# Chunked attention and expert layers on one core: another order for the first 20 microseconds of set-up

## The chip, the core and the metric

The kernel runs on one core of a Trainium2 chip. The core has a matmul engine (TensorE, in the profile PE, with the loading of its stationary operand as PEld), three engines for elementwise work (VectorE or DVE, ScalarE or ACT, GpSimd or POOL), and SyncE (SP), whose queue issues nearly all loads here. The metric is the device time of one execution in microseconds (us). The time before is 486.27 us, the median of three runs (484.25 to 487.78).

## The reference

Two parts follow each other. The first is attention in chunks of 32 tokens, with 16 tokens of context on the left, 8 on the right, and 8 memory keys and values for each head:

```python
B, H, S, D = 4, 8, 768, 64
for c in range(S // 32):
    l, r = max(0, c * 32 - 16), min(S, c * 32 + 32 + 8)
    k_full = np.concatenate([mem_k, k[:, :, l:r]], axis=2)
    v_full = np.concatenate([mem_v, v[:, :, l:r]], axis=2)
    s = D ** -0.5 * np.matmul(q[:, :, c * 32:c * 32 + 32], k_full.transpose(0, 1, 3, 2))
    a = np.exp(s - s.max(-1, keepdims=True))
    a = a / (a.sum(-1, keepdims=True) + 1e-9)
    out[:, :, c * 32:c * 32 + 32] = np.matmul(a, v_full)
```

The second takes the 3072 tokens with 512 features each, finds the best of 8 experts for each token (a softmax over x @ w_gate), places up to `capacity` tokens in each expert, computes relu(x @ w1) @ w2 for them (512 to 1024 to 512), and multiplies by the token's gate value.

## The kernel before

Attention works through 24 tiles of 128 tokens, two to a segment of 256 tokens. For each segment there is a key tile KW (two buffers, named kw in the profile), which holds for each chunk the 64 columns that a chunk of queries meets: 24 shared with the chunk before, 32 of its own, 8 of memory keys. Two heads share a tile: head parity 0 has rows 0 to 63, parity 1 rows 64 to 127, and the other half of each block of columns has to be zero. The value tile VW (two buffers, vw) is built in the same way, with a column of ones that gives the sum of the exponentials.

For each segment, queries and keys are loaded on SP's queue (`load_q` L357, `load_k` L368), turned by PE (`trans_q` L463, `trans_k` L475), and copied from PSUM to SBUF by ACT, in the first segment partly by DVE (L465, L479). `copy_k` copies the shared keys from chunk to chunk and into the next key tile (L496, L498), and in the first segment of a batch the eight keys that come before (L492). `fill_mem_k` copies the memory keys into both key tiles of a batch (L450); they come from preT, which `trans_pre` makes out of the loaded memory keys with eight small transposes on PE (L433) and four copies (L437). `load_v` (L397, L400) loads values into VW, and `fill_mem_v` (L426) copies memory values by DMA from the tile ME, which POOL builds out of the loaded memory values, memv (L167 to L172).

Each engine carries out its instructions in the order in which the program has them; no planner moves them. What is changed is the part between the first load and the loop over tiles. In it the unused halves are cleared: `zero_k` (L128) copies zeros from the tile pad into a key tile, `zero_v` clears half of a value tile (L135 by POOL, L137 by ACT) and sets its ones (L138). `dummy` (L150) issues matmuls on zeros (two entries of the profile for each). The order before is:

- SP: keys 0, queries 0 (each in two halves), memory keys with the eight first keys of each head (`load_mem`, L118 and L119), memory values (L123), keys 1, queries 1, values 0, memory rows of VW 0, keys 2, queries 2, memory rows of VW 1, values 1.
- PE: dummies, keys 0, queries 0, memory keys, 20 dummies, and then the loop: scores of tile 0 (`scores`, L509), keys 1, scores of tile 1, queries 1, the transposes of tile 0's exponentials (L533), scores of tile 2, keys 2, and the first value product (`value`, L550).
- DVE: clearing of KW 0, its half of keys 0, its half of queries 0, then `copy_k`, its half of `fill_mem_k`, the clearing of half of KW 1 (`zero_k(1, 0)`), and in the loop a half of `fill_mem_k(1)`, the maximum of tile 0 (L517), the subtraction (L520), and the shared keys of segment 1.
- ACT: clearing of half of VW 0, its halves of keys 0 and queries 0, the four copies of `trans_pre`, its half of the shared and the memory keys; in the loop the four copies of keys 1.
- POOL: half of VW 0, ME, the other half of KW 1 (L173), both halves of VW 1, and at the loop's start its half of `fill_mem_k(1)`, without which the scores of tile 2 can't start; then the constants of the routing (from L578).

The loop starts each tile with scores, then the transposes of the next segment, the exponentials, and the later stages of earlier tiles. The expert part comes behind attention and is not touched.

## Time and profile before

| | |
|---|---|
| median of three runs | 486.27 us (484.25 to 487.78) |
| the profiled execution's own time | 483.69 us |
| its span, first to last instruction | 481.8 us |
| PE busy | 458.3 us (95%) |
| DVE busy | 308.9 us (64%) |
| ACT busy | 232.6 us (48%) |
| POOL busy | 118.2 us (25%) |
| mean granted clock of PE | 0.993 |

The shares are means over the whole span. The set-up is the first 13 us, the attention loop goes on to about 135 us, and the experts take the rest. In the timeline a row gives the start, the time from the start of its first to the end of its last instruction, engine, line, operation, the tiles written and read, the sizes, the count of instructions, and in brackets the idle time before it with what ended it. Rows of one engine can overlap by some hundredths of a microsecond. Rows marked SPq are issues of DMAs, with the waits inside them; not the transfers.

### The profile page before, as it was taken

What the parts mean: (1) busy time and instruction counts of PE and PEld (TensorE: products, weight loads), DVE (VectorE), ACT (ScalarE), POOL (GpSimd) and SP (SyncE); (2) the same over time, 40 slices, a digit from 0 to 9 for tenths busy, and PEclk for the clock granted to TensorE, in tenths of its full rate; (3) what the DMA queues carried; (4) which work ended last, traced back from release to release, by engine and by line L of the source; (5) the groups of instructions that cost most, each with busy time, mean ns of one, the idle gap of its engine ahead of it and who ended that gap; (6) DMA issues with size and microseconds to landing.
All of it is one profiled execution on the core that took longest, in us unless ns stands there. A gap on an engine that the chain in (4) does not pass through costs nothing.

```text
span 481.8 us, 11847 instructions
## 1 busy us (share of the span) xinstructions
PE 458.3 (95%) x4317; PEld 386.9 (80%) x4317; DVE 308.9 (64%) x686; ACT 232.6 (48%) x423; POOL 118.2 (25%) x158
## 2 busy tenths in 40 slices
PE   7899999999999999979999999999999999899993
PEld 6777877878789897867777898899888878677782
DVE  5988899999869447565448257555624676674410
ACT  6587968889635235255345056244502544533200
POOL 8631245555543621201001100100021011020011
PEclk9899999999999999999999999999999999999998
DMA  9787788897976755365705554270414356430011
GB/s 214 150 216 189 184 209 245 249 246 186 230 252 236 263 167 193 105 224 180 237 34 181 173 190 133 88 267 16 164 53 149 123 187 229 163 131 3 1 42 44
DMA packets 79920, 78.85 MB, mean 164 GB/s; under 512 B 33394, under 2 KB 60142, under 8 KB 79792
## 3 DMA queue, kind: packets, MB, share of 16 engines
q1 hardware_dynamic: 74992, 62.33, 44.4%
q0 software_dynamic: 4800, 14.95, 8.1%
q8 instruction: 65, 1.06, 1.0%
q14 instruction: 63, 0.52, 0.3%
HBM read 61.25 MB, written 15.99 MB: 160 GB/s over the span
## 4 chain that ended last, share of the span: by engine, by line
PE 52%; DMA 18%; issue 13%; DVE 10%; ACT 2%; SPq 1%; POOLq 1%; DVEq 0%; ACTq 0%
PE ps L858 19%; DMA out_dram<-y,tok 13%; PE ps L948 13%; PE lgp L927 5%; DMA raw<-in_q_dram 3%; PE ps L834 2%; PE ps L550 2%; DVE vw L415 2%; PE ps L463 2%; PE ps L509 2%; PE ps L331 2%; ACT kw L479 1%; DVE m L517 1%; DVE d L520 1%; SPq L397 1%
## 5 line engine op out<-in xcount | busy, mean ns | idle before, releaser
L871 ACT ACTIVATE hhi<-ps 128x512 fp32r<-128x512 f32 x68 | 40.7, 599 | 148.6 <-PE ps L858 133.0
L955 POOL DMA_INDIRECT out_dram<-y,tok x28 | 32.3, 1155 | 273.3 <-DVEq L842 140.9
L872 DVE SCALAR_TENSOR_TENSOR hlo<-ps,hhi 128x512 fp32r<-128x512 f32 x68 | 47.0, 691 | 68.6 <-ACT hhi L871 65.7
L858 PE MATMUL ps<-xhi,w1hi 128*128 128x320 f32 (+3 forms) x288 | 59.5, 328 | 3.6 <-ACT w2hi L849 1.7
L948 PE MATMUL ps<-w2hi,hhi 128*128 128x512 f32 x152 | 60.9, 401 | 0.0
L948 PE MATMUL ps<-w2lo,hhi 128*128 128x512 f32 x152 | 59.8, 393 | 0.0
L948 PE MATMUL ps<-w2hi,hlo 128*128 128x512 f32 x152 | 59.4, 391 | 0.0
L858 PE MATMUL ps<-xhi,w1lo 128*128 128x320 f32 (+3 forms) x288 | 57.7, 322 | 0.0
L858 PE MATMUL ps<-xlo,w1hi 128*128 128x320 f32 (+3 forms) x288 | 57.7, 322 | 0.0
L858 PEld LDWEIGHTS ps<-xhi,w1hi 128*128 128x128 f32 x288 | 45.2, 188 | 8.3 <-issue 2.1
L858 PEld LDWEIGHTS ps<-xhi,w1lo 128*128 128x128 f32 x288 | 45.9, 188 | 2.9
L858 PEld LDWEIGHTS ps<-xlo,w1hi 128*128 128x128 f32 x288 | 45.9, 188 | 2.8
L954 DVE TENSOR_SCALAR y<-ps,xg 128x512 f32<-128x512 f32 x19 | 14.3, 751 | 51.6 <-PE ps L948 44.0
L850 DVE TENSOR_TENSOR w2lo<-raw,w2hi 128x512 fp32r<-128x512 f32 x64 | 41.2, 685 | 0.9 <-DVEq L919 0.6
L823 DVE TENSOR_TENSOR w1lo<-raw,w1hi 128x512 fp32r<-128x512 f32 x56 | 36.7, 684 | 2.7 <-DVEq L842 0.8
L822 ACT CAST w1hi<-raw 128x512 fp32r<-128x512 f32 (+1 forms) x72 | 37.1, 573 | 0.9
L849 ACT CAST w2hi<-raw 128x512 fp32r<-128x512 f32 x64 | 36.2, 617 | 1.6 <-DMA raw<-in_moe_w_dram 1.6
L838 ACT CAST xhi<-ps 128x512 fp32r<-128x512 f32 x34 | 19.8, 587 | 29.6 <-PE ps L834 26.3
L948 PEld LDWEIGHTS ps<-w2hi,hlo 128*128 128x128 f32 x152 | 28.6, 188 | 6.7
L948 PEld LDWEIGHTS ps<-w2hi,hhi 128*128 128x128 f32 x152 | 28.5, 188 | 6.7
L839 DVE TENSOR_TENSOR xlo<-ps,xhi 128x512 fp32r<-128x512 f32 x34 | 23.1, 689 | 16.7 <-ACT xhi L838 16.7
L948 PEld LDWEIGHTS ps<-w2lo,hhi 128*128 128x128 f32 x152 | 28.5, 188 | 5.8
(169 smaller groups left out, 814.6 us busy)
## 6 DMA issues: line engine op xcount, KB each, us to landing
raw<-in_moe_w_dram SPq DMA_DIRECT2D x15, 2048.0 KB
raw<-in_q_dram SPq DMA_DIRECT2D x11, 512.0 KB
raw<-in_k_dram SPq DMA_DIRECT2D x10, 512.0 KB
vw<-in_v_dram SPq DMA_DIRECT2D x49, 64.0 KB
xg<-x_d SPq DMA_DIRECT2D x3, 792.0 KB
vw<-in_v_dram SPq DMA_DIRECT2D x31, 72.0 KB
xg<-x_d SPq DMA_DIRECT2D x4, 528.0 KB
xg<-x_d SPq DMA_DIRECT2D x2, 1056.0 KB
```

The costliest lines, as they stand in the source:

```text
L822: self.nc.scalar.copy(out=hi[sl], in_=raw[sl])
L823: (eng or self.nc.vector).tensor_tensor(out=lo[sl], in0=raw[sl], in1=hi[sl].bitcast(F32), op=ALU.subtract)
L838: nc.scalar.copy(out=self.xhi[:, d:d + k, sl], in_=pv)
L839: nc.vector.tensor_tensor(out=self.xlo[:, d:d + k, sl], in0=pv, in1=self.xhi[:, d:d + k, sl].bitcast(F32), op=ALU.subtract)
L849: self.nc.scalar.copy(out=self.w2a[:, j], in_=self.raw2[:, j])
L850: self.nc.vector.tensor_tensor(out=self.w2b[j // 4][:, j % 4], in0=self.raw2[:, j], in1=self.w2a[:, j].bitcast(F32), op=ALU.subtract)
L858: self.nc.tensor.matmul(ps, a[:, d, fs], b[:, d, o:o + w], start=(i + d == 0), stop=(i == 2 and d == KD - 1))
L871: self.nc.scalar.activation(out=self.hhi[hs], in_=ps, func=AF.Relu)
L872: self.nc.vector.scalar_tensor_tensor(out=self.hlo[hs], in0=ps, scalar=0.0, in1=self.hhi[hs].bitcast(F32), op0=ALU.max, op1=ALU.subtract)
L927: nc.tensor.matmul(ps, a, b, start=start, stop=stop)
L948: self.nc.tensor.matmul(ps, a[:, f, t * P:t * P + P], b, start=(f == 0 and i == 0), stop=(f == KF - 1 and i == 2))
L955: nc.gpsimd.indirect_dma_start(out=self.out[:, :], out_offset=bass.IndirectOffsetOnAxis(ap=tok[:, t:t + 1], axis=0), in_=y, in_offset=None ...
```

## The change

The load of the memory keys goes ahead of the first queries on SP's queue. On PE the memory keys are turned before the queries, and 20 dummies become 6, behind them. `copy_k` is cut in two, `share_k` (shared keys) and `prior_k` (the eight keys before); in the set-up the shared keys are copied right behind `trans_k(0)`, the others behind `trans_pre`. Two of the four copies of `trans_pre` go from ACT to DVE, DVE's half of `fill_mem_k(0)` goes to POOL, and `zero_k(1, 0)` from DVE to ACT. On POOL the clearing of half of KW 1 and of ME comes first, and `zero_v(0, 1)` comes behind the memory keys. On SP keys 2 and queries 2 come ahead of the memory rows of VW 0, and values 1 ahead of the memory rows of VW 1. In the loop the order and the engines are as before.

```diff
         self.load_k(0)
+        load_mem()
         self.load_q(0)
-        load_mem()
         load_memv(0)
...
         zero_v(0, 0, nc.scalar.copy)
-        zero_v(0, 1, None)
         self.load_v(0)
-        self.trans_k(0)
-        self.trans_q(0)
-        self.trans_pre(pre)
-        dummy(20)
-        self.copy_k(0)
-        self.fill_mem_k(0)
-        zero_k(1, 0)
+        nc.gpsimd.memset(KW[1][64:P, :, :, 0, :].rearrange("p a c d -> p (a c) d"), 0.0)
         nc.gpsimd.memset(ME, 0.0)
         for par in range(2):
             nc.gpsimd.memset(ME[par * 32:par * 32 + 32, par, :, 64:65], 1.0)
+        self.trans_k(0)
+        self.share_k(0)
+        self.trans_pre(pre)
+        self.prior_k(0)
         for par in range(2):
             r = slice(par * 32, par * 32 + 8)
             nc.gpsimd.tensor_copy(out=ME[r, par, :, 0:64], in_=memv[r])
-        nc.gpsimd.memset(KW[1][64:P, :, :, 0, :].rearrange("p a c d -> p (a c) d"), 0.0)
-        self.fill_mem_v(0)
+        self.trans_q(0)
         self.load_k(2)
         self.load_q(2)
+        self.fill_mem_k(0)
+        dummy(6)
+        zero_k(1, 0, nc.scalar.copy)
+        zero_v(0, 1, None)
+        self.fill_mem_v(0)
+        self.load_v(1)
         zero_v(1, 0, None)
         zero_v(1, 1, None)
         self.fill_mem_v(1)
-        self.load_v(1)
...
         for j in range(2):
             for hf in range(2):
-                nc.scalar.copy(out=self.preT[...], in_=ps[...])
+                (nc.vector.tensor_copy if hf else nc.scalar.copy)(out=self.preT[...], in_=ps[...])
...
-            (self.nc.scalar.copy if n == 0 and not hf else (self.nc.gpsimd if n and not hf else self.nc.vector).tensor_copy)(
+            (self.nc.scalar.copy if n == 0 and not hf else (self.nc.gpsimd if not n or not hf else self.nc.vector).tensor_copy)(
                 out=kw[r, :, :, hf, 56:64], in_=self.pre_cols(0, b)[r, :, None, :].broadcast_to([64, 4, 8, 8]))
...
     def copy_k(self, n):
+        self.prior_k(n)
+        self.share_k(n)
+
+    def prior_k(self, n):
         nc = self.nc
         b, s = self.segs[n]
-        kw, kx = self.KW[n % NKW], self.KW[(n + 1) % NKW]
         if s == 0:
             for hf in range(2):
                 r = slice(hf * 64, hf * 64 + 64)
-                nc.vector.tensor_copy(out=kw[r, :, 0, hf, 16:24], in_=self.pre_cols(1, b)[r])
+                nc.vector.tensor_copy(out=self.KW[n % NKW][r, :, 0, hf, 16:24], in_=self.pre_cols(1, b)[r])
+
+    def share_k(self, n):
+        nc, s = self.nc, self.segs[n][1]
+        kw, kx = self.KW[n % NKW], self.KW[(n + 1) % NKW]
         for hf in range(2):
             r = slice(hf * 64, hf * 64 + 64)
             copy = nc.scalar.copy if n == 0 and not hf else (nc.vector if n <= 1 or hf else nc.gpsimd).tensor_copy
             copy(out=kw[r, :, 1:8, hf, 0:24], in_=kw[r, :, 0:7, hf, 32:56])
             if s < NSEG - 1:
                 copy(out=kx[r, :, 0, hf, 0:24], in_=kw[r, :, 7, hf, 32:56])
```

## The prediction

> **What bounds the kernel now.** I read the page first, for the share of the matmul engine, then the busy times of stretches of 12 us, then the chain of waits and the timeline of the first 24 us, where the whole change lies. The page's head and the stretches:

> ```profile
> span 481.8 us, 11847 instructions
> ...
> 0.00:12.00 12.00, 9.36 (x110) 8.03 (x110) 7.02 (x11) 7.73 (x12) 9.97 (x18) 1.00 0.92 214
> 12.00:24.00 12.00, 10.37 (x181) 8.80 (x185) 11.57 (x20) 6.93 (x12) 7.48 (x15) 0.86 0.71 151
> 24.00:36.00 12.00, 11.52 (x246) 9.55 (x239) 10.72 (x29) 10.75 (x17) 3.79 (x11) 1.00 0.83 216
> ```

> After the length the columns are PE, PEld, DVE, ACT and POOL busy, PE's clock, the share of the DMA engines and GB/s. From 24 us on PE and DVE are nearly full. Before that PE has 12.00-9.36 = 2.6 and 12.00-10.37 = 1.6 us of idle time, and its clock is below full in the second stretch, where DVE (11.57) is the full engine. What ends last there, from the chain of waits:

> ```profile
> 1.77 4.61 DMA raw<-in_q_dram
> ...
> 10.65 2.07 DVE kw L492
> ...
> 13.51 3.04 DVE kw L128
> ...
> 17.17 0.70 DVE m L517
> ```

> The set-up waits for the first queries, then DVE carries the path. Two DVE entries are far too long for what they do: the copy of a 64x32 block takes 2.07 us, and clearing half of the second key tile 3.04. Both are copies from SBUF to SBUF that lie beside a POOL clearing of the second value tile. The timeline, with POOL's rows first:

> ```profile
> 7.90 0.84 POOL L172 COPY ME<-memv 8x256 f32<-8x256 f32 x2 [1.12 <-DMA memv<-in_mem_v_dram]
> 8.80 1.80 POOL L173 MEMSET kw<- 64x2048 f32 x1
> 10.64 2.05 POOL L135 MEMSET vw<- 64x2340 f32 x1
> 13.23 2.23 POOL L135 MEMSET vw<- 64x2340 f32 x1
> 15.42 1.24 POOL L138 MEMSET vw<- 64x36 f32 x1
> 16.71 0.71 POOL L450 COPY kw<-preT 64x256 f32<-64x256 f32 x1
> ...
> 13.63 1.14 PE L509 MATMUL ps<-kw,qT 128*32 128x128 f32 x32 [1.93 <-DVE kw L450]
> 14.70 1.97 PE L475 MATMUL ps<-ident,raw 128*128 128x128 f32 x8
> 16.60 1.70 PE L509 MATMUL ps<-kw,qT 128*32 128x128 f32 x32
> 18.23 1.97 PE L463 MATMUL ps<-ident,raw 128*64 128x128 f32 x32
> 20.71 1.08 PE L509 MATMUL ps<-kw,qT 128*32 128x128 f32 x32
> 21.73 1.09 PE L475 MATMUL ps<-ident,raw 128*128 128x128 f32 x8
> 23.18 1.11 PE L550 MATMUL ps<-vw,pT 128*32 128x130 f32 x32
> ```

> The short DVE copy ends at 10.65+2.07 = 12.72, as POOL's clearing ends at 10.64+2.05 = 12.69; the DVE clearing has only 1.1 us left after 13.23+2.23 = 15.46. So a DVE copy within SBUF waits for a POOL clearing that began first. PE's first scores start at 13.63 after 1.93 us of idle time, and their maximum is taken only at 17.17, behind that DVE clearing. The first scores of the second segment (of 256 tokens; segment 1, as segments count from 0) start at 20.71. That is the point at which I compare, because from there PE and DVE are both full.

> **The change, part by part.** All times are on the clock of this trace.

> ```profile
> 2.87 0.50 SPq L118 DMA_DIRECT2D raw<-in_mem_k_dram  x1
> 3.88 0.70 SPq L123 DMA_DIRECT2D memv<-in_mem_v_dram  x2
> 14.71 0.39 SPq L368 DMA_DIRECT2D raw<-in_k_dram  x1
> 16.74 2.24 SPq L426 DMA_DIRECT2D vw<-ME  x2
> 19.04 6.22 SPq L397 DMA_DIRECT2D vw<-in_v_dram  x8
> 3.85 1.62 PE L475 MATMUL ps<-ident,raw 128*128 128x128 f32 x8
> 7.51 0.85 PEld L463 LDWEIGHTS ps<-ident,raw 128*64 128x64 f32 x16 [0.24 <-DMA raw<-in_q_dram]
> 8.54 0.68 PE L433 MATMUL ps<-ident,raw 32*128 32x32 f32 x8
> 9.15 2.55 PE L150 MATMUL ps<-pad 128*64 128x64 f32 x40
> 8.66 0.69 DVE L465 COPY qT<-ps 128x512 f32<-128x512 f32 x1 [1.75 <-PE ps L463]
> 13.11 0.37 DVE L450 COPY kw<-preT 64x256 f32<-64x256 f32 x1
> 18.50 0.57 DVE L496 COPY kw<-kw 64x672 f32<-64x672 f32 x1
> 2.04 2.14 ACT L137 COPY vw<-pad 64x2340 f32<-64x2340 f32 x1
> 9.25 1.09 ACT L437 COPY preT<-ps 64x128 f32<-64x128 f32 x4 [1.06 <-PE ps L433]
> 10.37 0.75 ACT L496 COPY kw<-kw 64x672 f32<-64x672 f32 x1
> 11.20 0.62 ACT L450 COPY kw<-preT 64x256 f32<-64x256 f32 x1
> 15.85 2.52 ACT L479 COPY kw<-ps 64x512 f32<-64x512 f32 x4 [4.03 <-PE ps L475]
> ```

> *Memory keys before queries.* On SP's queue the queries move behind two issues that took from 2.87 to 3.88. At most they come 3.88-2.87 = 1.0 us later; at least by the bytes, 0.131 MB at 214 GB/s = 0.6. A gain is excluded: nothing moves out of their way. I take 0.8, so the second half of the queries, which PE waited for until 7.51, comes at 8.3. The memory keys take the queries' place in the queue, so they are there by 1.77+4.61 = 6.4, and their eight transposes (0.68) fit into PE's wait after 3.85+1.62 = 5.5. The later loads keep their places and bytes.

> *Order on PE.* Query transposes ended at 8.54; now 8.54+0.8 = 9.3, DVE's copy of the second half (0.69) at about 10.1. The warming matmuls shrink from 40 to 12, 2.55*12/40 = 0.8 us, and lie beside that copy.

> *Key tile 0.* ACT leaves its key copies at about 6.3 (they don't depend on anything moved). The shared keys cost it 11.20-10.37 = 0.8, two quarters of the 1.09 for the transposed memory keys 0.5, its query copy runs at about 8.4 to 9.0, the memory columns 0.62: done at 9.7. DVE does the shared keys (0.57 and one short copy, POOL being without a clearing there), two copies from PSUM and the 64x32 blocks by 9.0. POOL's memory copies end at 8.74 as before (they wait for a load whose place is kept), then it does its new half of the memory columns, 0.71 by the POOL row at 16.71: 9.5. So the first scores start at about 10.2, when the queries' copy is done, instead of 13.63.

> *Clearing on ACT.* The 3.04 us leave DVE. ACT clears 64x2048, by its row for 2340 columns 2.14*2048/2340 = 1.9 us, from 9.7 to 11.6. Behind it wait ACT's four key copies of segment 1 (2.52), whose first PE block would be ready at about 11; so 0.6 at most, covered by DVE, which is busy with the first maximum until then. If that cover is gone it costs 0.6.

> *DVE.* Its first instruction of the loop is a memory-column copy (0.37), which finds POOL clearing from 9.5 and waits until 9.5+2.05 = 11.6. The first maximum then starts at about 12.3 instead of 17.17: 4.9 earlier.

> *POOL, which is late next.* All three value clearings still stand ahead of POOL's half of the memory columns of segment 1, at 16.71 in the trace. The first one went from the front to behind the wait for the memory values, and the 0.71 is new. From 9.5: three clearings with their columns of ones, at best 3*2.2 = 6.6, and 0.71, which ends at 16.8. Its conflicts with DVE come on top: DVE's memory column (0.37) and four shared copies of segment 1 (two of 0.57 and two short ones, about 1.5) can hold POOL for up to 1.9: 18.7. The shortest case is excluded by the row at 15.42, where a small memset beside a DVE copy took 1.24 us. I take 18.2, and scores of segment 1 from 18.3 instead of 20.71. **The sum is 20.71-18.3 = 2.4 us**, with ends of 2.0 (18.7) and 3.9 (16.8).

> [...] If each of POOL's clearings won against the four shared copies, the end of 18.7 would hold and the sum be 2.0, not my 18.2 and 2.4.

> *SP.* The same number of issues stands in the set-up; it ended at 19.04+6.22 = 25.26. The second value load no longer stands behind the memory rows of the second tile, whose issue took 2.24 with its wait for POOL. So SP ends between 0 and 2.2 us earlier, which agrees with the sum. Behind it the third key load and all later loads move with it. The first tile's memory rows now stand behind two loads of 0.5 MB each, of which below.

> From 20.7 us on, no instruction changes; the 2.4 us should stay. The profiled execution took 483.69 us, its span 481.8 and 1.9 around it: 481.3 by the sum. It lies 2.6 below the median of 486.27, so against the median the forecast is **483.9**.

> **The rivals.** *The clock falls again (485.4).* After 1.93 us of idle PE the clock went to half:

> ```profile
> 15.00:16.00 1.00, 1.00 (x6) 1.00 (x5) 1.00 (x1) 0.15 (x1) 1.00 (x2) 0.50 0.45 58
> ```

> [...] It cost 1.97-1.09 = 0.9 on key transposes and 1.70-1.08 = 0.6 on scores, 1.5 in all, while DVE was the path anyway. In the changed kernel PE runs scores, transposes and scores (1.1 each from 10.2) and query transposes (1.97) until about 15.5, then four transposes, and then waits for POOL's 18.2: again some 2 us idle, and now PE itself is late afterwards. 2.4-1.5 = 0.9 is left. For it: the same idle length. Against: the fall need not follow each time; the idle time before 6.4 brought none (1.00 in the first stretch).

> *All of it passes (481.4).* POOL is done at its early end, and later stalls shrink too, as loads start earlier; one such stall:

> ```profile
> 91.20 8.55 DMA raw<-in_q_dram
> ```

> Then DVE's 4.9 us are kept: 481.4. Against it: POOL's early end excludes every conflict.

> *Nothing passes (486.3).* That load at 91.20 is one of several on the chain; if the DMA engines set the pace there, what the start gains is given back. Against: their share of 0.83 at 24 to 36 leaves room. This is also the case in which the reordering doesn't do what it says.

> *Slower: memory rows behind the loads (488.8).* The two copies of memory rows into value tile 0 had been issued before the load at 14.71; now they follow two loads of 0.52 MB. The first value product (23.18) needs them, and PE takes its work in order, so the scores and products of the next tiles queue behind. Two loads at the 151 GB/s of that stretch take 6.9 us; from 14 that is 21, in time. If the rate were that of its worst parts, near 100, they'd take 10.5 and the product would start at 24.5 or later, 1.3 late; with the clock falling in that new wait, 1.5 more: some 2.5 slower. It decides where the rows land after 23.18. [...] No row here shows the order of these landings.

> **How the numbers follow.** Forecast 0.42, clock 0.22, all passes 0.16, nothing 0.10, slower 0.10. The likeliest is 483.9. One per cent is 4.9 us, about what can be told from no change here (three runs lay between 484.25 and 487.78). Faster by more: most of the third case, whose 4.9 is just at the bound, and the far end of the forecast with 3.9: 0.16. Slower by more (over 491.1): only the far end of the last case, and scatter: 0.07. Within: 0.77. The range runs from 481.0, a little past the third case, to 488.5, just short of the slower one; its own range for the forecast alone is 482.4 to 484.3.

> **What would show it.** First scores at about 10 and first maximum at about 12.3; no DVE clearing of the second key tile; POOL's memory columns of segment 1 ending near 18, and the second segment's scores right behind them, with PE idle for 2 us before. Wrong would be: scores of segment 1 waiting for something else than POOL, the first value product waiting for memory rows, or a shift at 24 us that is gone by 130.

## The result, and the profile after

The changed kernel takes 491.16 us (median of four runs, 490.51 to 492.63) against 485.26 us for the kernel before, run beside it (four runs, 484.23 to 487.78). The ratio is 1.0125, with a 95% interval from 1.009 to 1.016: **1.25% slower**, where 483.9 us, 0.5% less than the 486.27 known then, was forecast. Executions of a kernel that took far longer than its others (735.37 us in one below) enter no ratio. The profiled execution took 491.75 us with a span of 490.0, against 483.69 and 481.8: 8.2 us more between the first and the last instruction.

Nothing of this was lost in the set-up, where the whole reordering lies. From the page of the changed kernel, and then its busy times by stretches of 12 us (the columns are those of the table that the prediction shows):

```profile
span 490.0 us, 11790 instructions
...
PE 462.1 (94%) x4289; PEld 390.0 (80%) x4289; DVE 306.1 (62%) x686; ACT 233.7 (48%) x422; POOL 117.4 (24%) x159
...
q8 instruction: 65, 1.06, 0.9%
```

```profile
0.00:12.00 12.00, 10.20 (x80) 9.25 (x81) 7.15 (x15) 8.54 (x11) 8.64 (x17) 1.00 0.88 216
12.00:24.00 12.00, 11.12 (x221) 8.92 (x219) 9.77 (x16) 8.48 (x15) 8.92 (x18) 1.00 0.75 165
24.00:36.00 12.00, 9.71 (x197) 7.97 (x194) 9.64 (x26) 8.65 (x14) 2.81 (x8) 1.00 0.81 197
```

The page of the kernel before has, for the line with the engines' busy times:

```profile
PE 458.3 (95%) x4317; PEld 386.9 (80%) x4317; DVE 308.9 (64%) x686; ACT 232.6 (48%) x423; POOL 118.2 (25%) x158
```

From 12 to 24 us PE does 221 matmuls where it did 181, as the change meant it to. From 24 to 36 us it does 197 where it did 246: the lead is gone again. PE has 4317-4289 = 28 matmuls fewer in the whole program, and as many loads of its stationary operand: the 14 warming calls that were dropped, four PE instructions each, 56 in all. That number mattered more than the order.

The timeline of the changed kernel, the rows that answer to those of the prediction:

```profile
7.52 3.68 PE L465 MATMUL ps<-ident,raw 128*64 128x128 f32 x32
10.99 1.49 PE L150 MATMUL ps<-pad 128*64 128x64 f32 x12
12.41 1.15 PE L520 MATMUL ps<-kw,qT 128*32 128x128 f32 x32
18.25 1.45 PE L520 MATMUL ps<-kw,qT 128*32 128x128 f32 x32
22.14 1.10 PE L561 MATMUL ps<-vw,pT 128*32 128x130 f32 x32 [0.57 <-DMA vw<-ME]
31.53 1.06 PE L477 MATMUL ps<-ident,raw 128*128 128x128 f32 x8 [2.29 <-DMA raw<-in_k_dram]
34.59 1.08 PE L520 MATMUL ps<-kw,qT 128*32 128x128 f32 x32
127.40 1.11 PE L520 MATMUL ps<-kw,qT 128*32 128x128 f32 x31
...
13.89 0.69 DVE L528 TENSOR_REDUCE m<-ps 128x8 f32<-128x512 f32 x1
...
10.57 1.90 ACT L128 COPY kw<-pad 64x2048 f32<-64x2048 f32 x1
...
17.58 0.61 POOL L452 COPY kw<-preT 64x256 f32<-64x256 f32 x1
...
16.57 6.07 SPq L398 DMA_DIRECT2D vw<-in_v_dram  x8
24.31 1.82 SPq L123 DMA_DIRECT2D memv<-in_mem_v_dram  x2
26.23 0.39 SPq L369 DMA_DIRECT2D raw<-in_k_dram  x1
```

The same rows of the kernel before, as far as the prediction does not have them:

```profile
26.10 0.39 SPq L368 DMA_DIRECT2D raw<-in_k_dram  x1
...
30.47 1.06 PE L475 MATMUL ps<-ident,raw 128*128 128x128 f32 x8
33.98 1.08 PE L509 MATMUL ps<-kw,qT 128*32 128x128 f32 x32 [0.36 <-DVE kw L492]
127.60 1.11 PE L509 MATMUL ps<-kw,qT 128*32 128x128 f32 x31
```

The scores of segment 1 (tile 2) start at 18.25 instead of 20.71, right behind POOL's memory columns, which end at 17.58+0.61 = 18.19. Tile 3 is only 1.1 us ahead (23.03 against 24.10): the scores of tile 2 ran 1.45 us instead of 1.08, and PE waited 0.20 us for ACT and 0.57 us for the memory rows of VW 0. Tile 4 is 1.2 us ahead. Then the transposes of segment 3's keys wait 2.29 us for a load that was issued at 26.23, as before (26.10), and tile 5 starts 0.6 us later than before (34.59 against 33.98). At the last tile of attention 0.2 us are left (127.40 against 127.60). So attention ends where it ended, and the 8.2 us come behind it, in the expert part, whose code the change does not touch. Four stretches of 10 us there, first of the kernel before, then of the changed one:

```profile
200.00:210.00 10.00, 9.03 (x75) 8.61 (x74) 6.70 (x11) 6.31 (x12) 1.10 (x1) 1.00 0.83 281
210.00:220.00 10.00, 8.33 (x56) 7.16 (x55) 6.16 (x10) 4.36 (x9) 0.00 (x0) 1.00 0.51 169
370.00:380.00 10.00, 9.64 (x65) 9.15 (x64) 6.78 (x12) 6.08 (x11) 0.00 (x0) 1.00 0.73 268
380.00:390.00 10.00, 10.00 (x58) 8.01 (x57) 7.18 (x13) 6.25 (x12) 0.00 (x0) 1.00 0.38 121
```

```profile
200.00:210.00 10.00, 6.94 (x56) 6.49 (x55) 5.13 (x9) 4.35 (x8) 0.91 (x1) 1.00 0.87 278
210.00:220.00 10.00, 8.20 (x51) 7.24 (x50) 6.06 (x10) 4.93 (x9) 0.00 (x0) 0.87 0.35 103
217.00:221.00 4.00, 3.71 (x14) 3.08 (x14) 1.05 (x3) 0.59 (x1) 0.00 (x0) 0.57 0.61 143
370.00:380.00 10.00, 7.64 (x52) 7.24 (x51) 6.35 (x10) 4.45 (x8) 1.14 (x1) 1.00 0.74 250
380.00:390.00 10.00, 9.51 (x52) 9.23 (x53) 3.55 (x6) 3.43 (x7) 0.00 (x0) 0.83 0.14 50
381.00:385.00 4.00, 4.00 (x19) 4.00 (x18) 0.69 (x1) 0.60 (x1) 0.00 (x0) 0.57 0.08 30
```

From 200 to 210 us PE loses 9.03-6.94 = 2.1 us of busy time and 19 matmuls; from 370 to 380 us, 2.0 and 13. The clock falls twice, from 217.41 and from 381.25 us, each time from 1.00 to 0.50 for 3.41 us by the trace's records. The second fall follows the end of a stop of 2.85 us at 380.49; the first doesn't follow the stop near 206 us directly, but a later one of 1.80 us:

```profile
217.29 0.51 PE L938 MATMUL lgp<-w2lo,hhi 128*128 128x512 f32 x1 [1.80 <-issue]
```

In the kernel before the clock doesn't fall in the experts until their last 3 us. The 0.57 over 4 us agrees: (1-0.57)*4/0.5 = 3.4 us of it were at 0.50. What a fall costs is an estimate: by the ratio of the two clocks, 3.4 us at 0.50 stand for at least 1.7 at 1.00, so each fall costs up to 1.7 (eight key transposes of the kernel before took 1.97 us in a stretch where the clock went down to 0.50, and 1.09 at 1.00, a factor of 1.8). What PE waits for, from the timeline of the changed kernel around 206 us:

```profile
205.33 0.71 PE L869 MATMUL ps<-xhi,w1hi 128*128 128x256 f32 x4 [0.25 <-DVE hlo L883]
208.85 0.74 PE L869 MATMUL ps<-xhi,w1lo 128*128 128x256 f32 x4 [2.81 <-issue]
```

And of the kernel before at the same point of the program:

```profile
205.52 0.71 PE L858 MATMUL ps<-xhi,w1hi 128*128 128x256 f32 x4 [0.25 <-DVE hlo L872]
206.07 0.63 PE L858 MATMUL ps<-xhi,w1lo 128*128 128x256 f32 x4
...
214.07 0.33 PE L867 MATMUL ps<-pad 128*64 128x64 f32 x2 [1.67 <-issue]
```

PE stops in the middle of a row of matmuls for 2.81 us, and the releaser is "issue": no tile, no load and no other engine that this view knows of. (What moves beside it is looked at in the last experiment.) The kernel before has such stops too, at other points, here 1.67 us ahead of the matmuls on zeros at 214.07 (the program has them in the other arm of a branch, for where tokens are skipped). If all idle times of PE above 0.3 us behind 150 us are added up from the two timelines, it is 5.9 us before (6 of them) and 11.4 after (7 of them). The difference of 5.5, and two falls of the clock at 1.7, less the 0.2 that attention gained, make 8.7 us, where the span grew by 8.2; the 0.5 too much isn't traced further.

### The profile page after: what moved, and what is told of

Its sections match the earlier page's. It is cut to its first block, busy times and chain, and to the rows that moved or that the text cites. A ratio compares the mean times of both kernels' runs of the same rounds, so it can differ in the third digit from the quotient of the medians.

```text
span 490.0 us, 11790 instructions
## 1 busy us (share of the span) xinstructions
PE 462.1 (94%) x4289; PEld 390.0 (80%) x4289; DVE 306.1 (62%) x686; ACT 233.7 (48%) x422; POOL 117.4 (24%) x159
## 3 DMA queue, kind: packets, MB, share of 16 engines
q8 instruction: 65, 1.06, 0.9%
## 4 chain that ended last, share of the span: by engine, by line
PE 54%; DMA 19%; issue 14%; DVE 7%; ACT 2%; POOL 1%; POOLq 1%; SPq 0%; DVEq 0%; ACTq 0%
PE ps L869 18%; DMA out_dram<-y,tok 13%; PE ps L959 13%; PE lgp L938 5%; DMA raw<-in_k_dram 3%; PE ps L561 3%; PE ps L845 2%; PE ps L520 2%; PE ps L465 2%; DMA raw<-in_q_dram 2%; PE ps L332 1%; PE ps L616 1%; DMA vw<-ME 1%; DVE vw L416 1%; PE lgp L959 1%
## 5 line engine op out<-in xcount | busy, mean ns | idle before, releaser
L481 ACT COPY kw<-ps 64x512 f32<-64x512 f32 x46 | 28.8, 626 | 10.2 <-PE ps L477 8.9
```

Source lines behind the costliest of these rows:

```text
L481: (nc.vector.tensor_copy if n == 0 and hf else nc.scalar.copy)(out=kw[r, :, :, hf, 24 + j:56:2], in_=ps[j * 64:j * 64 + 64])
```

## The experiments

Three theories stood at the start. *Order* (rival B in the expectations): the new order of the set-up is itself the cause, through the loads that now start at other times and the memory rows behind two big loads, with something of it reaching the experts. *Warming* (rival C): the missing warming calls cost by themselves, at the start. *Position* (theory A): the cause is that PE's program has 56 instructions fewer ahead of the experts, so that everything behind lies at another place relative to the blocks in which, by this theory, PE's instructions are fetched. The page of the profile bears on this with the queue q8 of kind "instruction", which moved 1.06 MB in 65 packets, 16 KB each. In the first 140 us of the kernel before one of them starts on average for every 252 PE instructions of the profile (5034 for 20 packets), behind 150 us of the changed kernel one for every 76 (3439 for 45). That such a packet is a block of PE's instructions, of about 252 of them, is an estimate from the first of these figures; the packets themselves are looked at in the last experiment. The expert part has branches (tiles without tokens are skipped), attention has none.

### Both orders, with 20 and with 6 warming calls

The changed kernel with the 20 calls of the kernel before:

```diff
-        dummy(6)
+        dummy(20)
```

> The changed kernel with 20 warming matmuls instead of 6 behind the first queries, as many as before, so PE has as many instructions ahead of the experts as before. Theory A (code position): PE's stalls in the expert part come from where its instructions lie in the blocks of 16 KB that it fetches, and return to those of before: after 172 us no stall of 2.8 us, some 6 us of stalls in all instead of 11, clock not falling at 217 and 381; total 484 to 487 us. Rival B (time): the expert part is disturbed because attention's loads and releases come at other moments; then the stalls stay near 11 us and the total at 490 to 492. Rival C (fewer warming matmuls): the missing warming itself costs; it would show in the first 20 us alone, with a gain there, and leave the expert part at 490.

The kernel before with 6 calls, its order untouched:

```diff
-        dummy(20)
+        dummy(6)
```

> The kernel before with one edit, 6 warming matmuls instead of 20. Theory A: the expert part gets the stalls of the changed kernel (one of 2.8 us near 206, one near 378), total 489 to 492 us though nothing else of the change is there. Rival B: 485 to 487, stalls as before. Rival C: a slower first 20 us (clock low longer), up to 2 us, the expert part as before.

The times, as ratios to the kernel before (485.2 us, run beside them; for the changed kernel the 485.26 of the result), with 95% intervals:

| | 20 calls | 6 calls |
|---|---|---|
| order before | 1 | 1.0119 (1.0038 to 1.0199) |
| order after | 1.0012 (0.9977 to 1.0048) | 1.0125 (1.009 to 1.016) |

The loss goes with the 14 calls and not with the order. Dropping the calls alone makes the old order slower by as much as the whole change; with the calls put back, the new order can't be told from the old one. The timeline of the new order with 20 calls, at the point where the changed kernel stopped for 2.81 us:

```profile
205.84 0.63 PE L869 MATMUL ps<-xhi,w1lo 128*128 128x256 f32 x4
...
213.85 0.33 PE L878 MATMUL ps<-pad 128*64 128x64 f32 x2 [1.38 <-issue]
```

The stop is gone from there, and stands ahead of the matmuls on zeros, as in the kernel before. The old order with 6 calls:

```profile
206.53 0.72 PE L858 MATMUL ps<-xhi,w1hi 128*128 128x256 f32 x4 [0.25 <-DVE hlo L872]
207.09 0.28 PE L858 MATMUL ps<-xhi,w1lo 128*128 128x256 f32 x1
209.85 0.92 PE L858 MATMUL ps<-xhi,w1lo 128*128 128x256 f32 x3 [2.48 <-issue]
```

Here it has come to the place of the changed kernel, a matmul later. The sums of idle times above 0.3 us behind 150 us are 5.3 us for the new order with 20 calls, and 9.2 for the old one with 6, which also has two stretches at the clock of 0.50 (210.0 to 213.4 and 380.6 to 384.1 us), each behind a stop. Of its 7.3 us of span (489.1 against 481.8), 9.2-5.9 = 3.3 are stops and up to 3.4 the clock; its attention ended about 1 us later.

### The calls put back at another place

If it is the count of instructions ahead of the experts, it doesn't matter where they stand. So the set-up stays as in the changed kernel, with its 6 calls, and 14 pairs of small matmuls on four columns are put ahead of tile 12, in the middle of attention:

```diff
+        def fill(n):
+            ps = self.psum()
+            for _ in range(n):
+                nc.tensor.matmul(ps[0:64, 0:4], self.pad[:, 0:64], self.pad[:, 0:4], start=True, stop=True)
...
         for t in range(NTL):
             n = t // 2 + 1
+            if t == 12:
+                fill(14)
```

> The changed kernel with 14 small matmuls on zeros (4 columns each) added ahead of tile 12, so the set-up is as in the changed kernel and only the instruction count ahead of the experts is that of before. Theory A: stalls as before, 484.5 to 487 us. Rivals B and C: 490 to 492.

It took 485.59 us (ten runs), ratio 1.002 (0.9989 to 1.005): the loss is gone, with nothing changed in the first 60 us. So it isn't the warmth of PE at the start that was missing, nor anything in the set-up. The profile is of the longest of the ten (491.58 us); even there the idle times behind 150 us add up to 4.9 us, like those of the kernel before and of the new order with 20 calls.

### The same point, one block further

If it is the place within the blocks, and a block is the 252 instructions estimated above, then adding 200 must do nearly what leaving out 56 did: the two places differ by 200+56 = 256, four more than a block of that size. No run shows the exact size of a block. The kernel before, with 50 small calls of four PE instructions ahead of tile 12:

```diff
+            if t == 12:
+                fill(50)
```

> The kernel before with 50 small matmuls on zeros ahead of tile 12. [...] Theory A with blocks: the stalls are those of the changed kernel (one of 2 to 3 us near 210, one near 380), total 490 to 495 with 2 to 3 us for the added matmuls themselves. If only the number of instructions taken away mattered (or the warming), the expert part stays as in the kernel before, total 486 to 488.

It took 499.03 us against 486.14, ratio 1.0258 (1.0213 to 1.0303). That is more than was expected, since the added matmuls and a fall of the clock behind them (77 to 84 us) made attention 5.6 us longer. The other 12.9-5.6 = 7.3 us are in the experts (an estimate: the 12.9 are of medians, the 5.6 of two profiles): idle times of 9.5 us instead of 5.9, and a clock of 0.51 from 217 to 224 us, which costs up to 3.4 by the same estimate. The timeline, and the stretch behind:

```profile
215.08 0.71 PE L865 MATMUL ps<-xhi,w1hi 128*128 128x256 f32 x4 [0.25 <-DVE hlo L879]
218.67 1.22 PE L865 MATMUL ps<-xhi,w1lo 128*128 128x256 f32 x4 [2.88 <-issue]
```

```profile
217.00:224.00 7.00, 5.33 (x25) 5.33 (x26) 0.89 (x3) 1.25 (x3) 0.00 (x0) 0.51 0.62 215
```

The stop has come back between the same two groups of matmuls as in the changed kernel, with 2.88 us for 2.81. Two kernels whose counts of instructions differ by 256 stop at the same point; two that differ by 56 don't.

### Other amounts

With 28 and 42 small calls in the changed kernel, which are 14 and 28 calls past the place of the kernel before:

```diff
             if t == 12:
-                fill(14)
+                fill(28)
```

> The changed kernel with 28 small matmuls ahead of tile 12: PE's later code lies 14 times 4 instructions behind its place in the kernel before. Theory A: yet another set of stalls in the expert part, at the same sites or others, between 2 and 12 us in all; no theory gives the sign. Rival B: stalls as in the changed kernel, 11 us.

> The changed kernel with 42 small matmuls ahead of tile 12: PE's later code lies 28 times 4 instructions behind its place in the kernel before. Theory A: another set of stalls, between 2 and 12 us in all. Rival B: stalls as in the changed kernel, 11 us.

One execution each: 492.44 and 493.49 us. The added calls make attention longer, by 3.2 and 7.1 us, so the times say little; the idle times behind 150 us were 8.8 and 8.9 us, and stood at other points, for instance ahead of a matmul of the second layer with 28 calls:

```profile
189.13 0.50 PE L945 MATMUL lgp<-w2hi,hhi 128*128 128x512 f32 x1 [2.34 <-issue]
```

So the kernel before has a favourable place, and the changed kernel's is not the only one where the sum is high.

### The order on SP's queue

The changed kernel with SP's old order: memory rows of VW 0 ahead of keys and queries 2, values 1 behind the memory rows of VW 1. It keeps the 6 calls.

```diff
-        self.load_k(2)
-        self.load_q(2)
         self.fill_mem_k(0)
         dummy(6)
         zero_k(1, 0, nc.scalar.copy)
         zero_v(0, 1, None)
         self.fill_mem_v(0)
-        self.load_v(1)
+        self.load_k(2)
+        self.load_q(2)
         zero_v(1, 0, None)
         zero_v(1, 1, None)
         self.fill_mem_v(1)
+        self.load_v(1)
```

> The changed kernel with SP's old order in the set-up: memory rows of value tile 0 ahead of the third keys and queries, and the second values behind the memory rows of value tile 1. If the memory rows behind two loads ate the gain of the start, the first value product starts near 20.7 instead of 22.1 and waits for no memory rows, and the third key transposes at about 29 instead of 31.5; attention ends about 1 us earlier. If the second values' place was what mattered, SP waits for POOL's clearing and the third keys come as late as before (26), no gain. The expert part by theory A stays as in the changed kernel (same count on PE): total 489 to 491; by rival B anything from 484 to 492.

(The "third key" load of this text is that of segment 3, the fourth.) The ratio was 1.0114 (1.0015 to 1.0212), from three times between 487.38 and 493.94 us. Its timeline:

```profile
21.13 1.10 PE L561 MATMUL ps<-vw,pT 128*32 128x130 f32 x32
...
30.94 1.06 PE L477 MATMUL ps<-ident,raw 128*128 128x128 f32 x8 [2.63 <-DVE m L528]
```

The first value product comes 1.0 us earlier than in the changed kernel (22.14), and doesn't wait for memory rows. But other executions with the new order on SP's queue have it as early: 21.22 in the new order with 20 calls, after 0.23 us of waiting for memory rows, and 20.93 without the weight loads in the experts (below), with no such wait. So the memory rows behind the loads cost between nothing and 0.57 us. Segment 3's key transposes still come at 30.94, where about 29 was expected for an earlier attention, and the last scores at 127.71, no earlier than with the other order. The order on SP's queue is not what made the kernel slower.

### Making the gain of the set-up last

By the timeline, what gives the gain back is the load of segment 3's keys at 26 us. In this version it is issued ahead of values 1, with the 20 calls kept so that position plays no part; the later memory values come one tile later, to make room:

```diff
-        dummy(6)
+        dummy(20)
...
-        self.load_v(1)
...
-        self.fill_mem_v(1)
...
-            if t < 3:
-                load_memv(t + 1)
-            if t == 3:
+            if 0 < t < 4:
+                load_memv(t)
+            if t == 4:
...
                     if n + 2 < NS:
                         self.load_k(n + 2)
+                    if t == 0:
+                        self.load_v(1)
+                        self.fill_mem_v(1)
```

> The changed kernel with 20 warming matmuls (the instruction count of before on PE), and on SP's queue the fourth key load ahead of the second values, their memory rows and the later memory values (which go one tile later). Theory on the start: the gain of 2.5 us at tile 2 is lost at tile 5 because the fourth keys are issued at 26 us as before, behind the second values; now issued near 17 and landed by 24, the fourth segment's key transposes follow tile 4's scores without a wait, and attention ends 1.5 to 3 us earlier than in the kernel before: total 482 to 484.5. Rival: the second values or their memory rows come too late for tile 2's value product in turn, or the DMA engines give it back later: attention ends within 0.5 us of before, total 485 to 487.

> The kernel with 20 warming matmuls and the fourth keys moved ahead once more, for a narrower interval on whether it beats the kernel before. By its first profile attention ends 0.6 us earlier and the stalls of the expert part are 0.4 us shorter: ratio 0.996 to 0.999. If its place on PE or its start differ from run to run as much as that, 0.999 to 1.002.

The timeline:

```profile
15.91 0.39 SPq L370 DMA_DIRECT2D raw<-in_k_dram  x1
...
28.77 1.09 PE L478 MATMUL ps<-ident,raw 128*128 128x128 f32 x8
31.98 1.08 PE L521 MATMUL ps<-kw,qT 128*32 128x128 f32 x32
```

The load goes out at 15.91 instead of 26.23, the transposes at 28.77 no longer wait for it, and tile 5 starts 2.0 us earlier than in the kernel before (33.98). From tile 7 on some 1.3 us are kept, and 0.6 of them are left at the last tile (126.99 against 127.60), where 1.5 to 3 were expected. The ratios are 0.9976 (0.9944 to 1.0008) and, on another chip, where the kernel before took 498.79 us, 0.9967 (0.9927 to 1.0008). Both are 0.2 to 0.3% below 1, and neither interval excludes no change. The two versions that follow confirm what took the gain back: there too the transposes don't wait, and tile 5 starts at 32.06 and 33.60 (33.98 before the change). How much of it reaches the end of attention, and whether the kernel beats the one before, is not settled. The profile on the other chip also limits the rule of the place: with the same code its idle times behind 150 us were 9.8 us, at partly other points, so the place alone doesn't fix the stops.

The same version with 16 and with 24 calls, to see how fine the dependence is:

```diff
-        dummy(20)
+        dummy(16)
```

> The kernel with the fourth keys moved ahead, with 16 warming matmuls instead of 20: PE's later code lies 16 instructions (1 KB) ahead of its place in the kernel before. If stalls depend on the place finely, they come out between those of 20 (5.4 us) and of 6 (9 to 11 us), at the sites of one or the other: total 484 to 489. If a block edge must be crossed first, the stalls stay as with 20: 484 to 486.

> The same with 24 warming matmuls: PE's later code lies 16 instructions behind its place in the kernel before. Stalls between those of 20 (5.4 us) and of the place 14 matmuls further (8.4 us): total 484 to 489; as with 20 if no edge is crossed: 484 to 486.

(The 1 KB of the first text is 16*16/252 = 1.0, for 16 of the 252 instructions to a packet of 16 KB.) With 16 the ratio was 1.0107 (1.002 to 1.0193) and the idle times behind 150 us 9.1 us; with 24 it was 1.0066 (1.004 to 1.0093) and 7.1 us; with 20 they were 5.4 us. The last scores came at 127.96 and 127.43, within 0.4 us of the kernel before. So with four calls, 16 instructions, more or less the kernel was 0.7 to 1% slower than the one before: 20 is a narrow place.

### Without the weight loads in the experts

What makes such a stop 2 to 3 us long? In the changed kernel the stops at 206 and 377 us lie beside loads of tokens or of the next expert's weights. The transfers beside the first, from the queues of the changed kernel from 205.5 to 209 us (packets, MB, share of 16 engines):

```profile
q1 hardware_dynamic: 281, 0.98, 78.3%
q0 software_dynamic: 76, 0.25, 17.9%
q8 instruction: 1, 0.02, 1.6%
```

One packet of q8 moved in that time, beside 1.23 MB of data on engines that were 98% busy. This kernel leaves out the loads of the next experts' weights inside the expert part (it computes with old weights; the rest of the work stays):

```diff
-        if e + 1 < E:
-            nc.sync.dma_start(out=self.raw2, in_=self.w2[e + 1].rearrange("(k p) d -> p k d", p=P))
...
-        if e + 2 < E:
-            nc.sync.dma_start(out=self.raw1, in_=self.w1[e + 2].rearrange("(k p) f -> p k f", p=P))
```

> The changed kernel without the weight loads inside the expert loop (second-layer weights of experts 1 to 7 and first-layer weights of experts 2 to 7 aren't loaded, old ones are used in their place); PE's instructions are the same. If a stall is the fetch of a block of PE's instructions delayed by the big loads in the same DMA engines, the stalls near 206, 377 and 417 shrink to under 1 us each and the total falls to 480 to 484. If the fetch alone takes that long, whatever the engines carry, they stay at 1.5 to 3 us and the total at 489 to 492.

```profile
200.00:210.00 10.00, 6.72 (x52) 6.35 (x53) 6.15 (x10) 4.34 (x8) 0.98 (x1) 0.98 0.45 139
370.00:380.00 10.00, 10.00 (x67) 9.30 (x66) 5.75 (x10) 4.45 (x8) 0.98 (x1) 1.00 0.10 34
```

One execution, 484.83 us against 483.81 for the kernel before on that chip: 1.0 us more, where the changed kernel has 5.9. From 370 to 380 us the DMA engines are now at 0.10, PE is busy without a gap (7.64 in the changed kernel), and the clock stays at full. But from 200 to 210 us, where tokens are still loaded, a stop of 3.28 us is left, though the DMA engines were at 0.45. It stands between two matmuls on zeros, not at the changed kernel's point, so leaving out the loads (and the waits for them) may have moved PE's code by a few instructions. By this run alone the question would be open.

The packets of q8 answer most of it. For each stop the table gives the time at which such a packet starts, how long after it PE goes on, and how busy the DMA engines were in between:

| kernel | PE's stop, us | packet of q8 starts | to PE's next matmul | DMA engines |
|---|---|---|---|---|
| changed | 206.04 to 208.85 | 206.48 | 2.37 | 0.98 |
| changed | 215.49 to 217.29 | 214.59 | 2.70 | 0.03 |
| changed | 377.64 to 380.49 | 377.87 | 2.62 | 0.97 |
| before | 212.40 to 214.07 | 211.63 | 2.44 | 0.13 |
| new order, 20 calls | 212.47 to 213.85 | 211.37 | 2.48 | 0.09 |
| without weight loads | 206.04 to 209.32 | 206.69 | 2.63 | 0.08 |

The fourteen profiles of this case have 49 stops of PE over 1.1 us behind 150 us, and in 48 of them a packet of q8 had started 2.3 to 2.9 us before PE went on. Some 45 such packets lie in the last 330 us, so chance would bring about four of the 49 (an estimate). So these waits go with packets of the instruction queue, also where the profile names another releaser, as at 380.49 (DVEq L919). A stop lasts until 2.3 to 2.9 us behind the start of its packet, so its length depends on when it began: the stops of 2.8 to 3.3 us in the table began before their packet, the shorter ones 0.8 to 1.1 us behind its start. The traffic doesn't set it: 2.37 us with the engines at 0.98, 2.70 with hardly any. The packets themselves took 0.9 to 1.4 us; what fills the rest is open, and so is what sets when a packet starts. Without the weight loads packets started at 373.18 and 377.32 us and PE waited behind neither; nothing shows that the stop near 377 us went because a fetch became faster.

## Why the prediction was wrong

**The set-up** was read rightly in what bounds it. POOL's path was the term that set the gain: its memory columns of segment 1 were put at an end of 18.2 and ended at 18.19, and the scores of segment 1 were put at 18.3 and came at 18.25. So the sum of 2.4 us came out (2.46 measured, 20.71-18.25), and ACT's clearing took 1.90 for 1.9. That POOL's end agrees to a hundredth is luck. Its half of the first memory columns ended at 10.45 where 9.5 was worked out, as it had waited 1.49 us for preT; from there to its last copy it took 7.1 us where 8.0 was allowed. The conflicts that the prediction put on top of POOL's clearings held DVE instead (a shared copy took 1.93 us at 15.48). The prediction also has this the wrong way round: if POOL's clearings win, DVE's copies don't hold POOL, and its early end of 16.8 would stand, not 18.7. In two other executions with this set-up (with 42 small calls, and without the weight loads) POOL's copy ended at 17.41 and 17.24, and the scores of segment 1 started at 17.47 and 17.73.

**The first scores** were put at 10.2 and came at 12.41. The order of the transposes was right, but PE was slow: 32 query transposes took 3.68 us (1.97 elsewhere) and 12 warming matmuls 1.49 us where 0.8 was worked out, 1.9 times as long, which is near the 1.8 of the key transposes when the clock went down to 0.50 (1.97 for 1.09). The stretch from 0 to 12 us is printed with a clock of 1.00, but the trace of this execution has records of the clock only from 12.62 us on (from 4.27 in the kernel before); the 1.00 stands for no record, and that the clock was low there is inferred from the durations. That PE was slow for so long is not due to the new order: with the same set-up the records begin at 4.70 with 42 small calls, where the query transposes took 1.97 us and the first scores started at 9.56, and at 12.58 with 14, where they took 3.68. It delayed POOL through preT, and by the two executions above that cost 0.5 to 0.8 us at tile 2. Another term could fail too: without the weight loads DVE's copy of the eight keys before (64x32, L498) took 2.80 us at 8.89 beside POOL's first clearing, and the first scores started at 11.84. The first maximum moved with the scores, to 13.89 instead of 12.3. The 2 us of idle time that PE should have had before segment 1's scores weren't there either, as PE was late itself.

**SP's end** was put 0 to 2.2 us earlier. It was earlier by 25.26-24.31 = 0.95, and then the memory values (1.82 instead of 0.69) took this back, so segment 3's keys went out at 26.23 instead of 26.10. I had written that this range "agrees with the sum". It did not have to be compared with the sum, but with the next load that someone waits for. The term was 0, and so the lead ended at tile 5.

**The step that failed** is the sentence "From 20.7 us on, no instruction changes; the 2.4 us should stay". Both halves fell. The gain didn't stay: 1.4 of the 2.46 us were gone at tile 3, through longer scores and two short waits, and the wait of 2.29 us for segment 3's keys took the rest by 35 us. This alone would have made the case "nothing passes", 486.3, though by one load's issue and not by the pace of the DMA engines. And though no instruction changes, each of PE's instructions moves by 56 places. I priced the 14 dropped calls by what they take (0.8 us instead of 2.55, beside a copy) and not by what they shift. This is the 8 us: 5.5 of stops in the experts and up to 3.4 of clock.

**The rivals.** *The clock falls again* named the right price, 1.5 us for a fall, but put it in the set-up; in the changed kernel's profile it came twice, at up to 1.7, behind stops in the experts. In other executions it did come early: with 42 small calls PE was idle for 2.12 us ahead of segment 1's scores at 17.47, as this rival has it, and the clock fell at 18.35; in four others with the late keys it fell at 32 to 33 us, behind the wait for them. *Memory rows behind the loads*, the slower rival, came in this execution: its rows landed by 22.1, between the 21 and the 24.5 that were worked out, for a wait of 0.57 us. The 21 has the rows land behind both loads, and no run shows that order; they landed at 22.01, 6.17 us after their second issue started (15.84). The loss had another cause, and no rival named it. The chance of slower, 0.07, was thus too low by a whole mechanism. The profile before had shown such a stop, 1.67 us ahead of 214.07 with the releaser "issue". I didn't ask what these stops depend on.

In the kernels before and after, PE's stops over 1 us with the releaser "issue" stand in the experts alone, where the branches are. The stops shown here took 1.4 to 3.3 us, and the idle times above 0.3 us behind 150 us come to 5 to 11 us in a kernel of 485.

That the place of PE's instructions is the cause is shown by the runs: the loss went with the 14 calls in either order, went away when they were put back elsewhere, and came back with 200 instructions more. That PE waits for instructions in these stops is inferred from the packets, 48 of 49. Whether the branches have a part in it is not shown: every kernel here has them in the experts, and no run leaves them out.

## What to carry to other kernels

In this program 56 PE instructions dropped in the set-up made the experts slower, by 1.2% of the whole, and as many put back in the middle of attention took the loss away (ratio 1.002). Before two versions are compared, bring their counts of instructions on that engine to the same place (here by 14 calls on zeros), or the comparison may measure the place. Look for idle time whose releaser is "issue" (6.6 of the 11.4 us in the changed kernel), and for a packet of the instruction queue that starts 2.3 to 2.9 us before an idle time ends. A gain at the start is worth what the next load leaves of it, so follow the queue to the first load that someone waits for, and move that one too.
